# Splitting the pauses of a transform stage into short pieces, so that a second task's steps fall between them

## Chip, cores and metric

One NeuronCore of one Trainium2 chip. The metric is the device time of one execution in microseconds (us). Fast runs of the kernel before scatter by some 0.4% (1793.95 to 1801.04 us over 11 runs of one set of rounds), so two versions are compared in rounds on one chip.

In the profile PE is TensorE, PEld its weight loads, DVE VectorE, ACT ScalarE, POOL GpSimd, SPq the queue of the engine that issues most DMAs. "L646" is line 646 of the kernel.

## The reference, cut to what matters

The reference is the forward and backward pass of `x + A(layernorm(x)) + B(layernorm(x))`. `A` is a state-space convolution over 2048 steps and 576 channels, done with a Fourier transform. `B` is a gated feed-forward block of width 4608.

```python
K = jnp.einsum("dn,dnl,dn->dl", Cc, P, dB).real      # kernel of the convolution
Yf = rfft(u) * rfft(K)                               # y = irfft(Yf)[:L]
h = relu(x @ W_gate) * (x @ W_up);  out_B = h @ W_down
out, vjp = jax.vjp(f, ...);  grads = vjp(grad_out)   # all gradients are outputs
```

## The kernel before

Two programs are emitted side by side into the same engine queues. The *feed-forward* program (`ffn.gen`) has most of the matmuls (L244, L270, L298, L336, L352) and uses five PSUM tiles, `ps_mm`. The *transform* program (`s4.gen`) uses three PSUM tiles, `ps_s4`. Each is a generator that yields estimated microseconds. The main loop advances the transform generator until its sum has caught up with 0.9 of the feed-forward sum:

```python
    for us in ffn.gen(ln, final):
        ft += us
        ...
        while s4_open and stt < PACE * (ft - start):
            r = next(sgen, None)
            ...
                stt += r
```

So a "pause" is no instruction. A `yield 6.0` only means that some 6.7 us (6.0/0.9) of feed-forward instructions come next in the program.

Inside the transform program three pairs of tasks are merged by `both`: task `a` runs at its own pace, and task `b` gets a fixed share of the time `a` has used.

```python
    def both(self, a, wa, b, wb):
        ta = tb = 0.0
        for us in a:
            ta += us
            yield us
            while b is not None and tb * wa < ta * wb:
                r = next(b, None)
                ...
                    tb += r
                    yield r
        if b is not None:
            yield from b

    # gen(): the three pairs
    yield from self.both(self.p1(0, 4, 10.0), 68.0, self.params(pw), 45.0)
    yield from self.both(self.p2(0, pools, pw), 0.8 * W2, self.p1(1, 2, 3.0), W1)    # 320 : 60
    yield from self.both(self.p2(1, pools, pw), 0.8 * W2, self.p3(0, 2, 3.0), W3)    # 320 : 58
```

`p2` is the *first task* of the two long passes. For every 16 channels it emits a block of vector work and pauses, and then, for every 4 channels, it goes through smaller steps:

```python
                # ... 12 VectorE and 4 ScalarE instructions: sine and cosine, powers, A, B, X, XC ...
                yield 6.0
                for dd in range(x0, x0 + SX, DG):
                    v.tensor_tensor(vw(Y), Ap(0), Bp(1), op=ALU.mult)    # L881
                    v.tensor_tensor(vw(V), Ap(1), Bp(0), op=ALU.mult)    # L882
                    v.tensor_tensor(Y[:], Y[:], V[:], op=ALU.add)        # L883
                    yield 2.1
                    ...self.sums(...);  yield 0.8        # L932, then V L936 and Sm L937 on VectorE
                    ...self.turn(...)                    # L908 yield 0.3, L918 yield 0.4
```

`p1(1)` and `p3(0)` are the *second task*. Their steps are small. Each fills one PSUM tile (a first-stage step of `p1` two) with one or two matmuls (first stage L629, mixing L646, unmixing L656, last stage L687), copies it out on ScalarE or VectorE, and yields 0.15 to 0.7 (but for a gap of 3.0 at the start of a stage):

```python
    def mix(self, dst, src):
        for o in range(2):
            ps = self.ps()                               # one of three ps_s4 tiles
            for i in range(2):
                nc.tensor.matmul(ps[i * 64:(i + 1) * 64, :DH], lhsT=self.FM[:, o, :], rhs=src[:, i, :], ...)   # L646
            g.bal.copy(dst[:, o, :], ps[:, :DH], DH)     # ScalarE or VectorE, by a running balance
            if o == 0:
                yield 0.15
```

In the long passes the balance sent all 304 of these copies to ScalarE.

The framework orders the emitted instructions once more at build time. In the trace of the kernel before, for example, L862 of one block (643.19 us) stands on VectorE between L881 (641.99) and L882 (643.79) of another, which the source emits one right after the other.

## Time and profile before

| | before |
|---|---|
| time, median of 3 (range) | 1796.94 us (1796.20 to 1797.74) |
| PE busy | 1710 of 1792 us, 95% |
| VectorE, ScalarE busy | 1318, 1188 us |
| PE idle in the two long passes | about 33 us of 1174 us |

First, four lines of the profile page of the kernel before: the span; busy time of each engine with its instruction count; PE's busy tenths in 40 slices; and the shares of the engines in the chain that ended last.

```profile
span 1792.2 us, 41927 instructions
...
PE 1710.2 (95%) x16306; PEld 1183.1 (66%) x16449; DVE 1318.2 (74%) x2867; ACT 1188.1 (66%) x2736; POOL 204.9 (11%) x246
...
PE   7989988999999999999999999999999998999998
...
PE 64%; DVE 22%; ACT 6%; DMA 5%; issue 3%; SPq 0%; POOL 0%; ACTq 0%; DVEq 0%; POOLq 0%
```

PE is busy in nearly every slice and makes up 64% of the chain. (This trace lacks 143 matmul records, 16306 of 16449, so 1710 us is slightly low.) The next view gives busy time by stretch. After the stretch and its length come the busy time of PE, PEld, DVE, ACT and POOL, then the granted PE clock, the DMA share and GB/s.

```profile
core 0: us, PE busy (x) PEld busy (x) DVE busy (x) ACT busy (x) POOL busy (x), PEclk, DMA share, GB/s
...
96.00:296.00 200.00, 179.12 (x1437) 116.24 (x1448) 145.50 (x335) 138.94 (x336) 16.55 (x22) 0.97 0.95 300
296.00:880.00 584.00, 569.86 (x5832) 400.71 (x5879) 443.19 (x867) 408.07 (x928) 86.77 (x90) 1.00 0.72 191
880.00:1470.00 590.00, 571.27 (x5800) 400.76 (x5846) 505.42 (x1057) 401.75 (x897) 73.39 (x78) 1.00 0.69 175
```

96 to 296 us is the first pair, the rest the two long passes. PE is idle for 20.9, 14.1 and 18.7 us (length less busy). Only these stretches run through `both`, so this is all that the change can reach.

This is the timeline near one long pause in the kernel before (start, duration, engine, line, output<-input; in brackets the engine's idle time and its releaser):

```profile
654.01 0.31 PE L646 MATMUL ps_s_10652<-b_ug,FM 128*64 128x288 bf16 x2
...
654.16 0.29 PE L646 MATMUL ps_s_10656<-b_ug,FM 128*64 128x288 bf16 x2
654.28 0.29 PE L646 MATMUL ps_s_10660<-b_ug,FM 128*64 128x288 bf16 x2
...
655.63 0.42 ACT L68 CAST s_ug<-ps_s_10652 128x288 bf16<-128x288 f32 x1
...
656.11 0.31 PE L646 MATMUL ps_s_10664<-b_ug,FM 128*64 128x288 bf16 x2 [0.78 <-ACT s_ug L68]
```

Three mixing tiles stand almost together. The copy of the first (655.63) comes late on ScalarE, since ScalarE was busy without a gap from 653.50 us with two of the block's activations and three feed-forward copies, and the fourth tile, which needs that buffer, leaves PE idle for 0.78 us. Here are some of PE's waits in the long passes (303 to 1468 us): who waited for whom, total us, times, longest:

```profile
PE ps_mm L298 <- DVE T L256: 2.6, 3, 1.3
PE ps_s_10499 L908 <- ACT fC_10464 L68: 2.3, 1, 2.3
...
PE ps_s_17526 L646 <- ACT fC_17493 L68: 1.6, 1, 1.6
...
PE ps_mm L270 <- DVE T L256: 1.2, 1, 1.2
...
PE ps_s_10664 L646 <- ACT s_ug L68: 0.8, 1, 0.8
...
PE ps_mm L298 <- DVE T L261: 0.7, 3, 0.3
```

`ps_s` waits at L629, L646 and L656 are the second task's; `ps_mm` waits are the feed-forward program's. Over the passes the second task's sum to 6.9 us, the first task's (L908, L918, L932) to 8.0. (Such sums take the waits that the view lists, each over 0.15 us.) The longest single wait, 2.3 us at L908, is counted as the first task's, since a matmul of the first task waits; but what it waits for is a ScalarE copy of a second-task tile (`fC`). At 640.9 us ScalarE ran out of work and stood for 3.04 us at the block's negated copy, and the `fC` copies came after that.

### The profile page before, as it was taken

How to read it: one execution, taken by the hardware profiler on the slowest of the kernel's cores; microseconds unless marked ns; L12 is line 12 of the kernel's file. 1: busy time of each engine (PE TensorE's matmuls, PEld its weight loads, DVE VectorE, ACT ScalarE, POOL GpSimd, SP SyncE). 2: the span in 40 equal slices, each digit the busy share in tenths (PEclk: the TensorE clock that was granted, in tenths of full speed). 3: DMA queues.
4: the chain of work that ended last, by engine and by line, in shares of the span. 5: the costliest groups of instructions: out<-in, count | busy, mean ns of one | idle time of the engine just before them, and what ended most of it. 6: DMA issues, size and time to landing. Idle time of an engine off the chain costs nothing.

```text
span 1792.2 us, 41927 instructions
## 1 busy us (share of the span) xinstructions
PE 1710.2 (95%) x16306; PEld 1183.1 (66%) x16449; DVE 1318.2 (74%) x2867; ACT 1188.1 (66%) x2736; POOL 204.9 (11%) x246
## 2 busy tenths in 40 slices
PE   7989988999999999999999999999999998999998
PEld 5665556667567666766766766766676675676676
DVE  7575884677889788678787889889978963972541
ACT  5875874686588577568468658747857845864651
POOL 0200012012022011012101101101111100110000
PEclk9999999999999999999999999999999999999999
DMA  8799989678568656866857857866776578995873
GB/s 294 263 325 305 337 228 297 199 183 241 178 137 219 195 149 149 234 183 148 227 157 185 233 157 141 211 186 154 178 189 153 108 214 260 259 289 157 269 239 100
DMA packets 239003, 373.30 MB, mean 208 GB/s; under 512 B 49490, under 2 KB 153428, under 8 KB 237268
## 3 DMA queue, kind: packets, MB, share of 16 engines
q1 hardware_dynamic: 212836, 304.09, 52.8%
q0 software_dynamic: 24384, 51.92, 18.9%
q10 hardware_dynamic: 1584, 14.60, 2.2%
q8 instruction: 129, 2.11, 0.5%
q14 instruction: 70, 0.57, 0.1%
HBM read 233.10 MB, written 137.43 MB: 207 GB/s over the span
## 4 chain that ended last, share of the span: by engine, by line
PE 64%; DVE 22%; ACT 6%; DMA 5%; issue 3%; SPq 0%; POOL 0%; ACTq 0%; DVEq 0%; POOLq 0%
PE ps_mm L298 18%; PE ps_mm L244 15%; PE ps_mm L352 11%; PE ps_mm L336 8%; PE ps_mm L270 3%; DVE V L936 2%; DVE T L261 2%; DVE Sm L937 2%; DVE V L882 2%; DVE Y L883 2%; DVE Y L881 1%; DVE rg L254 1%; PE ps_mm L370 1%; DMA gT<-in_gT_dram 1%; DVE X L862 1%
## 5 line engine op out<-in xcount | busy, mean ns | idle before, releaser
L298 PE MATMUL ps_mm<-wf,T 128*128 128x288 bf16 x3456 | 481.1, 287 | 7.6 <-DVE T L256 2.6
L298 PEld LDWEIGHTS <-T 128*128 128x128 bf16 x3456 | 324.2, 98 | 97.8 <-issue 13.7
L68 ACT CAST osx<-ps_mm 128x288 bf16<-128x288 f32 x682 | 260.4, 428 | 50.0 <-PE ps_mm L298 47.2
L311 POOL DMA_DIRECT2D acc_dram<-osx x160 | 139.0, 869 | 1026.4 <-ACT osx L68 588.2
L352 PEld LDWEIGHTS <-rows 128*128 128x128 bf16 x1536 | 146.1, 98 | 96.0 <-issue 1.6
L270 PEld LDWEIGHTS <-T 128*128 128x128 bf16 x1728 | 127.0, 98 | 85.7 <-DVE T L256 4.6
L254 DVE SCALAR_TENSOR_TENSOR rg<-rg,ps_mm 128x512 bf16<-128x512 bf16 x144 | 98.3, 683 | 112.7 <-PE ps_mm L244 73.7
L244 PE MATMUL ps_mm<-xT,wd_151 128*128 128x512 bf16 x710 | 179.2, 379 | 0.8 <-issue 0.3
L244 PE MATMUL ps_mm<-gT,wd_152 128*128 128x512 bf16 x700 | 175.5, 379 | 0.8 <-DMA gT<-in_gT_dram 0.6
L244 PE MATMUL ps_mm<-xT,wd_150 128*128 128x512 bf16 x593 | 164.9, 379 | 11.8 <-DMA xT<-xT_dram 1.6
L270 PE MATMUL ps_mm<-ident_bf,T 128*128 128x128 bf16 x1728 | 157.1, 220 | 4.7 <-DVE T L256 1.6
L336 PE MATMUL ps_mm<-rows,hN 128*128 128x144 bf16 x2304 | 158.7, 227 | 0.0
L336 PEld LDWEIGHTS <-hN 128*128 128x128 bf16 x2304 | 148.3, 98 | 8.1 <-issue 5.4
L68 ACT CAST obw<-ps_mm 128x384 bf16<-128x384 f32 x103 | 49.2, 478 | 146.2 <-PE ps_mm L352 114.2
L352 PE MATMUL ps_mm<-dgN,rows 128*128 128x384 bf16 x768 | 136.8, 326 | 1.0 <-DMA rows<-xs_dram_141 1.0
L352 PE MATMUL ps_mm<-duN,rows 128*128 128x384 bf16 x768 | 135.6, 326 | 0.0
L253 ACT ACTIVATE rg<-ps_mm 128x512 bf16<-128x512 f32 x144 | 86.9, 604 | 52.2 <-PE ps_mm L244 50.3
L68 ACT CAST dhb<-ps_mm 128x512 bf16<-128x512 f32 x141 | 83.8, 594 | 49.5 <-PE ps_mm L244 47.7
L261 DVE TENSOR_TENSOR T<-dhb,rg 128x1024 bf16<-128x1024 bf16 x141 | 101.1, 717 | 18.6 <-ACT dhb L68 17.8
L244 PEld LDWEIGHTS <-wd_150 128*128 128x128 bf16 x720 | 66.0, 97 | 62.3 <-issue 3.7
L244 PEld LDWEIGHTS <-wd_151 128*128 128x128 bf16 x720 | 65.2, 98 | 60.0 <-issue 3.2
L244 PEld LDWEIGHTS <-wd_152 128*128 128x128 bf16 x705 | 63.4, 98 | 58.6 <-issue 1.6
(2506 smaller groups left out, 3042.9 us busy)
## 6 DMA issues: line engine op xcount, KB each, us to landing
acc_dram<-osx POOLq DMA_DIRECT2D x176, 288.0 KB, 5.2
gT<-in_gT_dram SPq DMA_DIRECT2D x48, 640.0 KB, 6.2
xT<-xT_dram SPq DMA_DIRECT2D x44, 640.0 KB, 5.7
rows<-in_gq_dram SPq DMA_DIRECT2D x48, 576.0 KB, 4.2
wf<-in_Wf_dram ACTq DMA_DIRECT2D x11, 1296.0 KB, 8.9
ex_dram<-exs SPq DMA_DIRECT2D x36, 320.0 KB, 4.7
ex<-ex_dram SPq DMA_DIRECT2D x36, 320.0 KB, 4.3
out_dram<-obw SPq DMA_DIRECT2D x96, 96.0 KB, 2.6
```

Source lines behind the costliest of these rows:

```text
L68: self.nc.scalar.copy(out, in_)
L244: nc.tensor.matmul(ps[:], lhsT=w[:, k, fs], rhs=rhs[:, k, :], start=(k == 0), stop=(k == NK - 1))
L253: nc.scalar.activation(rg, ps_g[:], ACT.Relu)
L254: nc.vector.scalar_tensor_tensor(upm, rg, 0.0, ps_u[:], op0=ALU.is_gt, op1=ALU.mult)
L261: nc.vector.tensor_tensor(T[:, 1:3], dhb.unsqueeze(1).to_broadcast([P, 2, JS * P]), ru[:], op=ALU.mult)
L270: nc.tensor.transpose(out=pt[:, j, :], in_=src[:, j * P:(j + 1) * P], identity=g.ident_bf[:])
L298: nc.tensor.matmul(ps[:, cs], lhsT=lt, rhs=rh, start=(i == 0), stop=(i == len(mms) - 1))
L311: nc.gpsimd.dma_start(g.acc_dram[:, t, :, :], o[:], accum_op=ALU.add)
L336: nc.tensor.matmul(ps[:, ft * 144:(ft + 1) * 144], lhsT=self.hN[:, st, ft * P:(ft + 1) * P], rhs=gq[:, st, :], start=(st == 0), stop=(st = ...
L352: nc.tensor.matmul(ps[:, :Fc], lhsT=xs[:, st, 0:P], rhs=src[:, st, :], start=(st == 0), stop=(st == ST - 1))
L882: v.tensor_tensor(vw(V), Ap(1), Bp(0), op=ALU.mult)
L883: v.tensor_tensor(Y[:], Y[:], V[:], op=ALU.add)
```

## The change

The intent: a long pause of `a` is cut in pieces of about 1 us, so that `b` is paid after each piece and not in one go after the pause.

```diff
     def both(self, a, wa, b, wb):
 
         ta = tb = 0.0
-        for us in a:
+        for us in (p for us in a for p in [us / max(1, round(us))] * max(1, round(us))):
             ta += us
             yield us
             while b is not None and tb * wa < ta * wb:
```

A pause of 6.0 becomes six of 1.0, 2.1 becomes two of 1.05, 10.0 ten of 1.0. Sums and instructions stay.

## The prediction

> **What bounds the kernel now.** TensorE: the first table of the page has PE busy 1710 of 1792 us (95%), VectorE 1318, ScalarE 1188; the granted clock is 0.995. At most 82 us are idle PE time. By stretches (the view of busy time per window) PE is idle 15 us before 96 us, 21 us from 96 to 296 (first transform beside the parameter task), 33 us from 296 to 1470 (two kernel-generating passes, each beside a transform), 14 us after. Only the two middle stretches run code that goes through `both`.
>
> **What the change does.** No instruction is added or removed. A pause is only a number in the pacing of the emission: a pause of 6.0 (36 of them, one after each block of 16 columns) becomes six of 1.0, the 144 of 2.1 two of 1.05, the 10.0 gaps ten of 1.0. Sums stay, so stages should begin and end where they did. What moves is the second task's steps. Before, after a 6.0 pause it owed 6.0*60/320 = 1.1 us and paid it in one go, 3 to 5 small steps. After, it owes 0.19 us per piece and pays about one 0.15 step each, beside the block's roughly 10 us of VectorE work (pieces of 0.49 to 0.90 us).
>
> **Gain and cost on the critical path.** A bunch makes PE wait where a fourth matmul finds the transform's three psum buffers not yet evicted. Near 654 us the timeline shows it: a row of mixing matmuls, then PE idle 0.78 us for a ScalarE copy (0.42 us each). Over 296 to 1470 us PE's waits ahead of the second task's matmuls sum to 6.9 us (mixing 3.3, first stage 2.4, unmixing 1.3): all that spreading wins directly. The first task's own matmuls wait 8 us, the feed-forward ones 10 us, mostly for VectorE's T and ScalarE; these may shift either way.
> Against it: the steps now fall just behind the block's VectorE burst, where ScalarE waits for VectorE (the sine 31 us over 27 waits, the negated copy 23 us over 22; up to 4 us at once). It takes copies in order ([...] the trace agrees: near 644 us copies stand behind a negated copy that waited 3.0 us, and PE waited 2.3 us). A step in that hole holds a psum buffer longer. I expect half of the 6.9 us won, 0 to 4 us lost again, and in the first stretch 2 us either way.
>
> **Prediction.** 1794 us, 8 times in 10 between 1784 and 1806; faster by over 2%: 2%, within 2%: 95%, slower by over 2%: 3%.
>
> **What would show it.** Same instruction counts (but for copies moved between ScalarE and VectorE); stage boundaries within 10 us; second-task PE waits in 296 to 1470 us down from 6.9 to 3 or 4 us; shorter runs of adjacent second-task matmuls; ScalarE's waits for the sine argument and the negated copy about as before; PE busy still 1710 us.
>
> **What would make it wrong.** Copies are shared out by a running balance in order of emission, and the trace's VectorE order (blocks mixed with steps) is not the program's; a small shift can put many copies behind a blocked engine. If ScalarE is stuck with second-task copies, PE waits grow by over 10 us. If the feed-forward waits on VectorE come from the bunches, the gain could reach 12 us.

## The result and the profile after

The changed kernel took 1797.8 us in the median of 6 runs (1794.71 to 1800.27), the kernel before 1797.23 us in the same rounds (1794.78 to 1799.02). The ratio is 1.0003 with a 95% interval of 0.999 to 1.0016: no difference.

The same lines of the page, after:

```profile
span 1794.1 us, 42082 instructions
...
PE 1722.6 (96%) x16449; PEld 1184.1 (66%) x16449; DVE 1319.2 (74%) x2867; ACT 1188.9 (66%) x2736; POOL 203.9 (11%) x246
...
PE   7989988999999999999999999999999998999998
...
PE 62%; DVE 20%; DMA 8%; ACT 6%; issue 3%; SPq 1%; POOL 0%; ACTq 0%; DVEq 0%; POOLq 0%
```

Busy time by stretch, after:

```profile
96.00:296.00 200.00, 178.94 (x1429) 115.59 (x1427) 144.47 (x333) 139.03 (x335) 16.48 (x22) 0.97 0.94 298
296.00:880.00 584.00, 574.34 (x5854) 399.56 (x5852) 442.42 (x866) 407.73 (x928) 83.88 (x89) 1.00 0.72 191
880.00:1470.00 590.00, 575.33 (x5884) 402.26 (x5882) 505.74 (x1056) 402.10 (x897) 75.33 (x80) 1.00 0.69 175
```

The stages lie where they did, and VectorE's and ScalarE's counts are the same. That PE's busy time is 12 us higher is mostly an effect of records: this trace has all 16449. The feed-forward matmuls of the two traces cannot be compared by busy sums. A second trace of the kernel before, with 94 more PE records in the passes than the first, showed 1136.4 us busy there against 1129.2, and this one shows 1138.7.

The same place in the stage, after (mixing tiles of the same block):

```profile
651.23 0.31 PE L646 MATMUL ps_s_10576<-b_ug,FM 128*64 128x288 bf16 x2
...
652.88 0.31 PE L646 MATMUL ps_s_10592<-b_ug,FM 128*64 128x288 bf16 x2
...
654.34 0.31 PE L646 MATMUL ps_s_10618<-b_ug,FM 128*64 128x288 bf16 x2
...
655.79 0.31 PE L646 MATMUL ps_s_10636<-b_ug,FM 128*64 128x288 bf16 x2
```

The four tiles now stand 1.4 to 1.7 us apart and none waits. The intent was met. PE's waits in the long passes, after:

```profile
PE ps_mm L298 <- DVE T L256: 3.4, 4, 1.3
PE ps_mm L270 <- DVE T L256: 2.1, 2, 1.9
PE ps_mm L298 <- DVE T L261: 1.6, 5, 0.6
PE ps_s_10499 L908 <- ACT fC_10464 L68: 1.6, 1, 1.6
...
PE ps_s_9449 L646 <- DVE V L936: 1.2, 1, 1.2
...
PE ps_s_15659 L629 <- ACT fA_15603 L68: 1.1, 1, 1.1
```

The second task's waits fell, and waits of feed-forward matmuls for VectorE's `T` rose. Sorted and summed over the passes, with the second profiles described below:

| profile | built PE order | second task | first task | feed-forward (for VectorE) | sum | length of passes |
|---|---|---|---|---|---|---|
| before | before | 6.9 | 8.0 | 11.9 (7.5) | 26.7 | 1162 |
| before, again | before | 6.5 | 8.0 | 11.2 (7.5) | 25.7 | 1163 |
| only the first pair split | before | 7.0 | 8.4 | 12.6 (7.5) | 27.9 | 1165 |
| after | after | 4.3 | 6.8 | 12.5 (10.0) | 23.7 | 1163 |
| after, again | after | 3.7 | 6.0 | 12.6 (10.0) | 22.3 | 1159 |

The rows of one order agree within 1.4 us for each kind of wait. From one order to the other the second task's waits fall by 2.8 us (means 6.8 and 4.0), the first task's by 1.7 (1.2 of it waits for `fC` copies, so for second-task tiles again), and the feed-forward ones rise by 0.7 (those for VectorE by 2.5; a wait for a load of `rows`, 0.5 to 2.0 us in each of the three profiles of the order before, is absent from the two after). Net, 3.8 us less waiting, 0.2% of the time. The timed rounds of the result (interval from 0.999) exclude a gain of more than 0.1%. So the mechanism acts, its size is at the edge of what can be measured, and part of it comes back as feed-forward waits.

The granted clock adds scatter of the same size. The first profile of the changed kernel holds one place in the passes where it fell: 0.69, 0.50, 0.50 and 0.61 in the four us from 719 to 723, after waits of PE of 0.76, 1.20 and 0.38 us between 716.1 and 719.9 us. As an estimate (1 less the granted clock, summed over the passes) that is 1.7 us of PE time lost. In the second profile of the kernel before, PE waited once for 2.25 us, up to 648.9 us, and the clock was 0.50 from 650 to 653 us; in the first profile the same wait, 2.26 us up to 645.0 us, left it at 1.00. The profile with only the first pair split holds one such place too, the second of the changed kernel none. Since it fell on both orders, nothing here ties it to the change.

### The profile page after: what moved, and what is told of

Read it like the earlier page. It is cut to its first block, busy times and chain, and to the rows that moved or that the text cites. A ratio compares the mean times of both kernels' runs of the same rounds, so it can differ in the third digit from the quotient of the medians.

```text
span 1794.1 us, 42082 instructions
## 1 busy us (share of the span) xinstructions
PE 1722.6 (96%) x16449; PEld 1184.1 (66%) x16449; DVE 1319.2 (74%) x2867; ACT 1188.9 (66%) x2736; POOL 203.9 (11%) x246
## 4 chain that ended last, share of the span: by engine, by line
PE 62%; DVE 20%; DMA 8%; ACT 6%; issue 3%; SPq 1%; POOL 0%; ACTq 0%; DVEq 0%; POOLq 0%
PE ps_mm L298 17%; PE ps_mm L244 14%; PE ps_mm L352 11%; PE ps_mm L336 7%; PE ps_mm L270 3%; DVE V L936 2%; PE ps_mm L370 2%; DVE V L882 1%; DVE T L261 1%; DVE Sm L937 1%; DVE Y L883 1%; DVE Y L881 1%; DVE rg L254 1%; DVE X L862 1%; DMA ex_dram<-exs 1%
## 5 line engine op out<-in xcount | busy, mean ns | idle before, releaser
L298 PE MATMUL ps_mm<-wf,T 128*128 128x288 bf16 x3456 | 484.5, 287 | 9.6 <-DVE T L256 3.4
L298 PEld LDWEIGHTS <-T 128*128 128x128 bf16 x3456 | 324.2, 98 | 98.1 <-issue 10.7
L352 PEld LDWEIGHTS <-rows 128*128 128x128 bf16 x1536 | 145.7, 98 | 94.6 <-issue 1.5
L244 PE MATMUL ps_mm<-xT,wd_150 128*128 128x512 bf16 x720 | 180.3, 379 | 4.0 <-ACT xT L153 1.6
L244 PE MATMUL ps_mm<-xT,wd_151 128*128 128x512 bf16 x720 | 179.9, 379 | 0.0
L244 PE MATMUL ps_mm<-gT,wd_152 128*128 128x512 bf16 x705 | 176.0, 379 | 0.7 <-DMA gT<-in_gT_dram 0.7
L352 PE MATMUL ps_mm<-dgN,rows 128*128 128x384 bf16 x768 | 137.4, 326 | 0.0
L352 PE MATMUL ps_mm<-duN,rows 128*128 128x384 bf16 x768 | 136.6, 326 | 0.0
L244 PEld LDWEIGHTS <-wd_150 128*128 128x128 bf16 x720 | 66.1, 97 | 62.0 <-issue 3.7
L244 PEld LDWEIGHTS <-wd_151 128*128 128x128 bf16 x720 | 65.2, 98 | 61.0 <-issue 3.1
L244 PEld LDWEIGHTS <-wd_152 128*128 128x128 bf16 x705 | 63.3, 98 | 59.0 <-issue 2.1
```

The costliest lines, as they stand in the source:

```text
L244: nc.tensor.matmul(ps[:], lhsT=w[:, k, fs], rhs=rhs[:, k, :], start=(k == 0), stop=(k == NK - 1))
L298: nc.tensor.matmul(ps[:, cs], lhsT=lt, rhs=rh, start=(i == 0), stop=(i == len(mms) - 1))
L352: nc.tensor.matmul(ps[:, :Fc], lhsT=xs[:, st, 0:P], rhs=src[:, st, :], start=(st == 0), stop=(st == ST - 1))
```

## The experiments

Theory one: bunches of second-task steps cost PE waits for PSUM tiles that are not evicted; spreading removes such waits, but at three buffers the kernel before had few left. Rivals: the build-time order and the queues swallow bunches whatever their size; or spreading does win, and loses it again in the hole behind the vector block, where ScalarE waits for VectorE (30.7 us in 27 waits for the sine argument in the kernel before).

A static count from the built PE orders helps below: how often four second-task tiles start within 1 us of feed-forward matmul work (L629, L646 and L656 tiles; a feed-forward matmul counted at its spacing in the trace, 0.216 us for L244, 0.122 for L298, 0.163 for L352). I call these *crowded places*. No expectation uses this count, so what it explains below it explains after the fact. Before has 11, the changed kernel none. (A recount from the traces gives the same order of the kernels and numbers up to 9 lower; 0 stays 0.) In the kernels that I counted the built order (but for single runs of four, in the kernel served at 1.0 us and in the one with one task after the other) never puts more than three second-task tiles in a row, or two when there are two PSUM tiles, however many steps the source emits at once. Runs of three number 20 before and 1 after.

### The kernels unchanged, profiled again (before_again, after_again)

No edit. One profile each.

> The kernel before, unchanged, profiled a second time: how much the PE waits of 296 to 1470 us differ between two profiles of one program. If they repeat within 1 us in total (26.8 us, of them 6.9 ahead of second-task matmuls), the drop to 4.35 and the rise of the feed-forward waits by 2 us in the changed kernel are real; if they differ by 2 us or more, they are noise.

> The changed kernel, unchanged, profiled a second time. In the two long passes (303 to 1467 us) the first profile shows second-task PE waits of 4.3 us and feed-forward waits of 13.1 us, 10.1 of them for VectorE; three profiles of the PE order of before showed 6.5 to 7.0 and 7.5. If the shift from the one to the other is real, this repeats within 0.7 us.

Measured: 1798.29 us and 1794.82 us (single runs, state unknown). The waits are in the table above: 6.5 against 6.9, and 3.7 against 4.3 for the second task; 7.5 and 7.5, 10.0 and 10.0 for VectorE. (The 13.1 and 10.1 in the expectation are an earlier sum of the waits that the table has as 12.5 and 10.0.) So the shift between kinds of waits belongs to the order, not to noise.

### Only the first pair split (split_first)

```diff
-    def both(self, a, wa, b, wb):
+    def both(self, a, wa, b, wb, split=False):
-        for us in a:
+        for us in (p for us in a for p in ([us / max(1, round(us))] * max(1, round(us)) if split else [us])):
-            yield from self.both(self.p1(0, 4, 10.0), 68.0, self.params(pw), 45.0)
+            yield from self.both(self.p1(0, 4, 10.0), 68.0, self.params(pw), 45.0, True)
```

> Pauses split only in the first pair (first transform beside the parameters). The built PE order is the same as before, so theory one (what counts is only where an instruction stands in its engine's queue, a pause is nothing in itself) expects a ratio within 0.1% of 1 and PE waits of 96 to 296 us at 20 us as before. The rival (the split frees that stretch of some of its 21 us) expects 3 us or more less there.

Measured: ratio 1.0005 (0.9989 to 1.0021), 1797.78 us. PE was idle for 20.3 us from 96 to 296 us, before for 20.9: as theory one expected. The built PE order is the same as before, instruction for instruction. The orders of VectorE, ScalarE and the issuing queue differ in a few lines. In emission the parameter task started about 9 us of pacing earlier (after a pause of 1.0, not of 10.0), yet its first load did not. DMA issues before, then after the full change:

```profile
90.19 0.32 SPq L559 DMA_DIRECT2D s_dram<-d_o_1218  x1
92.30 0.33 SPq L571 DMA_DIRECT2D raw<-in_par_dram  x1
```

```profile
90.21 0.32 SPq L559 DMA_DIRECT2D s_dram<-d_o_1218  x1
92.33 0.33 SPq L571 DMA_DIRECT2D raw<-in_par_dram  x1
```

The load `raw` stands in the issuing queue behind a store of transform constants, `d_o_1218`, and it is issued at 92.3 us in both. In the kernel before, that store waited 1.3 us for the ScalarE copy that fills its tile, and `raw` then 1.7 us for the store. The queue's order up to there is the same, so there was nothing that it could have overtaken. The pause was here only a position among the other instructions of the same queue; where none lay between, moving had no effect.

### Only the long pauses split (split_long)

```diff
-        for us in a:
+        for us in (p for us in a for p in ([us / round(us)] * round(us) if us > 5.0 and wa > 300.0 else [us])):
```

> Only the 36 pauses of 6.0 in the long passes are split in six; those of 2.1, 3.5 and the 10.0 gaps stay whole. If the long pauses are the part that matters, its waits look like those of the changed kernel (second task 4 to 5 us, feed-forward 12 to 14 us); time within 3 us of before either way. If the gain is in the short pauses, second-task waits stay near 6.9 us.

Measured: ratio 0.9987 (0.997 to 1.0004), 1794.51 us: the same. Second-task waits fell to 2.1 us (below the 4 to 5 expected), first-task 7.3, feed-forward 12.2 (9.0 for VectorE), sum 21.6; crowded places 0. So the 36 long pauses hold the whole effect on the second task. It was the lowest mean of all versions run, but the interval holds 1. It also allows a gain of 0.3%, some 5 us.

### The opposite: serve the second task late (bunch1, bunch2, bunch4)

```diff
             ta += us
             yield us
+            if b is not None and (ta * wb - tb * wa) / wa < (4.0 if wa > 300.0 else 0.0):
+                continue
             while b is not None and tb * wa < ta * wb:
```

and the same with 2.0 and 1.0 in place of 4.0.

> The opposite of the change in the two long passes: the second task is served only when it is owed 4.0 us (about once per block of 16 columns), then all at once, so runs of 10 or more small steps. Theory one (a bunch costs PE a psum wait of some tenths of a us to a us, about 7 us in all) expects second-task PE waits up from 6.9 to 15 to 30 us and the time up by 8 to 25 us. The rival (the reordering at build time and slack of the queues swallow bunches whatever their size) expects the same time within 3 us.

> As the run that served the second task at 4.0 us owed (it took 2.2% more), but at 2.0 us owed. In the built PE order the second task's runs never exceed three psum tiles in any kernel (three buffers); runs of exactly three number 1 in the changed kernel, 20 before, 43 here and 43 at 4.0. If the cost of bunches is proportional to their size, 2.0 us should cost about half of the 42 us, 15 to 25 us over before; if it is a threshold (the buffers and queues swallow small bunches), under 10 us, with second-task PE waits under 15 us.

> The second task is served when 1.0 us is owed, in both kinds of pauses (before: 1.1 us after the long pauses, 0.4 after the short ones). Known so far: 4.0 us owed costs 42 us, 2.0 costs 17, the mix of before 0 against the finest pieces. A cost in proportion to the size puts 1.0 at about 8 us (ratio 1.004 to 1.006). A threshold near 1 us (three buffers and the queued feed-forward work swallow the bunch) puts it under 4 us (ratio below 1.0025), with second-task PE waits under 12 us.

| kernel | crowded places | second-task waits | sum of waits | clock lost (estimate) | passes | time, ratio (95% interval) |
|---|---|---|---|---|---|---|
| after | 0 | 4.3 | 23.7 | 1.7 | 1163 | 1.0003 (0.999 to 1.0016) |
| before | 11 | 6.9 | 26.7 | 0 | 1162 | 1 |
| served at 1.0 us | 47 | 16.8 | 39.3 | 6.8 | 1181 | 1.0075 (1.0057 to 1.0094) |
| served at 2.0 us | 57 | 25.7 | 37.3 | 5.1 | 1179 | 1.0095 (1.0081 to 1.0109) |
| served at 4.0 us | 78 | 36.5 | 53.6 | 10.2 | 1205 | 1.0219 (1.0196 to 1.0243) |

The medians were 1814.34, 1813.56 and 1839.03 us. The rival that bunches are swallowed is refuted: they cost up to 2.2%. At 4.0 us I had expected less: second-task waits of 15 to 30 us (they were 36.5) and 8 to 25 us of time (it was about 39). At 2.0 us the cost, about 17 us, lies in the range that goes with the size. At 1.0 us it was about 13.5 us (0.75% of 1798.6), far over a threshold's 4 and more than the 8 of a cost in proportion to the size, though the interval's low end, 1.0057, just reaches into that range (1.004 to 1.006).

What follows the time better than the size owed, at 1.0 and 2.0 us, is the count of crowded places. From before to 1.0 us, 36 more of them cost 13.5 us, 0.37 us each; to 2.0 us, 46 more cost 17 us, again 0.37 each; to 4.0 us, 67 more cost 39 us, 0.59 each. This is all time, not waits alone: at 1.0 us the profiled passes are 18 us longer than the mean of the three profiles of the order before, of which 12.5 us are waits and, as an estimate, 5 to 7 us are clock. As an estimate from the 0.37 us, the 11 of the kernel before are worth 4 us, in line with the 3.8 us of waits that left it, but more than the 1.8 us (0.1%) of gain that the timed rounds allow. The change found few bunches because most of the first task is not long pauses: of about 382 us that one `p2` yields, 18 × 6.0 = 108 are, 28%. The rest is yielded in steps of at most 2.1 (but for two of 3.5), after which no more than about 0.4 us of second-task work is owed. Serving at 1.0 us gathered that rest too.

At 4.0 us the waits are no longer for PSUM tiles alone. PE's waits there (300 to 1510 us):

```profile
PE ps_s L629 <- ACT fA L68: 9.9, 6, 2.7
PE ps_s L687 <- DMA bC<-C_dk: 8.1, 6, 2.1
PE ps_s L646 <- DMA b_k<-A_k: 5.8, 1, 5.8
...
PE ps_s L656 <- DVE pr_z L672: 4.8, 8, 1.1
```

The tasks' loads (`bC`, `b_k`), which a dense bunch reaches before they have landed, and products that VectorE has not finished come on top. The lower clock, which costs time at 1.0 and 2.0 us too (an estimated 6.8 and 5.1 us, table above), is easiest to see here. Busy time in stretches of 4 us around one such bunch; the third number from the right is the granted clock:

```profile
844.00:848.00 4.00, 2.19 (x14) 0.84 (x11) 1.11 (x2) 2.03 (x5) 0.00 (x0) 1.00 0.97 211
848.00:852.00 4.00, 2.61 (x34) 2.20 (x35) 1.93 (x4) 1.59 (x4) 0.00 (x0) 0.81 0.85 262
852.00:856.00 4.00, 4.00 (x30) 2.01 (x29) 2.33 (x5) 2.34 (x4) 0.00 (x0) 0.76 0.85 247
```

Two waits of 1.1 and 2.1 us for loads, and PE then runs at 0.81 and 0.76 of its clock in the mean of 4 us; in steps of 1 us the clock is 0.75 from 850 to 851 us, 0.50 to 853 and 0.55 to 854. The kernel before shows 1.00 in every us of the passes in its first profile.

### Pay the second task before the pause (pay_first)

```diff
             ta += us
-            yield us
+            if wa < 300.0:
+                yield us
             while b is not None and tb * wa < ta * wb:
                 ...
+            if wa > 300.0:
+                yield us
```

> In the two long passes the second task is paid its share before each pause and not after it, unsplit: bunches as long as before, but just behind the block's VectorE burst, where ScalarE waits for VectorE. If the hole behind the burst is what eats the gain of spreading, second-task PE waits rise from 6.9 by 10 us or more, and the time by 8 to 20 us. If the place does not matter, waits stay at 5 to 9 us and the time within 3 us.

Measured: ratio 1.0017 (1.0001 to 1.0034), 1800.61 us; crowded places 14; second-task waits 7.3 us, first-task 4.1, feed-forward 15.2 (11.8 for VectorE). The 8 to 20 us of the hole behind the vector block did not come. What moved instead is the feed-forward program's wait for VectorE, by 4.3 us. This, like the 2.5 us of the change, fits second-task products standing earlier in VectorE's queue, ahead of `T` (the second task's copies all ran on ScalarE here too); no run takes that apart.

### Two PSUM tiles for the transforms (two_psum_before, two_psum_after)

```diff
-    g.psum_mm = pool("psum_mm", 5, space=PSUM)
-    g.psum_s4 = pool("psum_s4", 3, space=PSUM)
+    g.psum_mm = pool("psum_mm", 6, space=PSUM)
+    g.psum_s4 = pool("psum_s4", 2, space=PSUM)
```

applied to the kernel before and to the changed one.

> The kernel before with two psum banks for the transforms and six for the feed-forward work. If bunches cost time through psum buffers that are not yet evicted, one buffer less makes them dearer: second-task PE waits up from 6.9 to 12 to 25 us, time up by 5 to 25 us. If buffers are not what limits, the time stays within 3 us.

> The changed kernel with two psum banks for the transforms. Theory one (spreading saves psum waits, but at three buffers there is too little left to save) expects it 4 us or more faster than the kernel before with two banks. The rival (spreading does not act through psum waits) expects the two within 2 us.

Measured: 1831.32 us, ratio 1.019 (1.0176 to 1.0204), and 1819.73 us, ratio 1.0127 (1.0113 to 1.014); the intervals are apart, and against each other spreading is 0.6% faster (1.0127/1.019 = 0.9938). With one buffer less the very same edit wins 11 us. The loss of 34 us unsplit is more than the 5 to 25 expected. (Both kernels also have a sixth feed-forward tile, and their feed-forward waits fell to about 4 us, so what the lost buffer costs by itself is probably more than the ratios show.) PE's waits in the passes with two tiles, unsplit and then split:

```profile
PE ps_s L918 <- DVE V L936: 16.1, 16, 2.6
PE ps_s L908 <- DVE V L936: 6.1, 12, 1.5
PE ps_s L629 <- ACT fA L68: 2.1, 5, 0.9
...
PE ps_s L656 <- ACT s_k L68: 1.7, 2, 1.4
```

```profile
PE ps_s L918 <- DVE V L936: 19.2, 15, 2.5
PE ps_s L908 <- DVE V L936: 4.3, 7, 1.5
...
PE ps_s L629 <- ACT fA L68: 0.6, 3, 0.2
...
PE ps_s L656 <- ACT fC L68: 0.4, 1, 0.4
```

The second task's waits fell from 7.7 to 2.1 us in sum, and those of the first task, 29.3 and 29.5 us, did not. So my expectation of where the cost would show was wrong: the second task's waits barely rose with two tiles (6.9 to 7.7); it is the first task's turning (L918) that waits, for VectorE's `V L936`, which reads the tile to be freed (16.1 us in 16 waits unsplit). The profiled runs were 7.2 us apart (spans 1825.5 and 1818.3), 5.6 of them in these waits (40.8 and 35.2 in sum); the rest of the 11 us of the medians is not located. The clock is not the reason: it lost an estimated 3.4 us in the passes unsplit and 5.1 split.

### One task after the other (one_after_other)

```diff
-                yield from self.both(self.p2(0, pools, pw), 0.8 * W2, self.p1(1, 2, 3.0), W1)
-                yield from self.both(self.p2(1, pools, pw), 0.8 * W2, self.p3(0, 2, 3.0), W3)
+                yield from self.p1(1, 2, 3.0)
+                yield from self.p2(0, pools, pw)
+                yield from self.p3(0, 2, 3.0)
+                yield from self.p2(1, pools, pw)
```

> No interleaving of the two tasks in the long passes: the transform of half 1, then the kernel pass of half 0, then the transform back of half 0, then the kernel pass of half 1, same pace in sum. The transform alone then runs over five times as dense, with buffers for two loads only, so I expect waits for its DMA loads and psum of 20 to 60 us and the time up by 1 to 4%. If even this costs under 0.5%, order between the tasks hardly matters at all.

Measured: ratio 1.0253 (1.023 to 1.0276), 1842.19 us. As expected, PE waits for the dense transform's loads (6.5 us for `bC`, 5.9 for `b_ug`) and for evictions of its tiles (L629 9.4, L646 6.0). In 296 to 444 us, where the transform of half 1 runs alone, the granted clock was 0.93. An estimated 15 us of its passes are lost clock, against 0 or 1.7 in the order before. Merging the tasks at all is worth 45 us; splitting the pauses as the change does is worth 1.8 us at most.

### An attempt to go below both (after_deep)

The changed kernel with nine buffers and loads ahead, in place of five, for the last stage of the first transform, where PE waits 6 us for `bC`:

```diff
-            bp = self.pool(c, f"p1_c{hf}", n + 1, "right")
+            bp = self.pool(c, f"p1_c{hf}", n + 1, "right")
+            cp = self.pool(c, f"p1_cc{hf}", 9 if n == 4 else n + 1, "right")
-                Ct = bp.tile([P, 2, 1, DH], BF16, name="bC1")
+                Ct = cp.tile([P, 2, 1, DH], BF16, name="bC1")
-            Sx, cs = ..., Ahead(load_c, ST, n + 1)
+            Sx, cs = ..., Ahead(load_c, ST, 9 if n == 4 else n + 1)
```

> The changed kernel, with nine buffers and nine loads ahead in place of five in the third stage of the first transform, where PE waits 6 to 7 us for loads that stand in the queue behind weight loads. If those waits are on the critical path they fall below 2 us and the time by 3 to 6 us against the changed kernel (ratio to before 0.997 to 0.999); if PE only waits elsewhere for the same transfers, the time stays within 2 us.

Measured: ratio 0.9994 (0.9979 to 1.0009), 1795.11 us: the same. PE's waits for loads there, in the changed kernel (second profile) and then in this one:

```profile
PE ps_s L687 <- DMA bC<-C_dk: 6.2, 5, 2.0
```

```profile
PE ps_s L687 <- DMA bC<-C_dk: 3.8, 1, 3.8
...
PE ps_mm L352 <- DMA rows<-xs_dram: 1.9, 1, 1.9
PE ps_s L687 <- DMA Sx<-s_dram: 0.5, 1, 0.5
```

The wait for `bC` fell by 2.4 us but did not go. A wait of 0.5 us for `Sx` is new, and one of 1.9 us for the feed-forward program's own `rows`. The three add up to 6.2 us again, as if the wait had moved; but the three profiles of the order before show `rows` waits of 0.5 to 2.0 us as well, so that part may be scatter. The DMA engines were 0.94 busy in the mean from 96 to 296 us in the changed kernel, which fits; that bandwidth is the cause was not tested apart. No version is clear of the kernel before on the fast side.

## Why the prediction was right

The time, 1797.8 us, lies in the range of 1784 to 1806, and "within 2%" held. That alone proves little: the range is 22 us wide, and the whole effect that the text argues for is 3.5 us won and 0 to 4 lost. The central value, 1794 us, stood for a gain of some 3 us; the rounds show 0.6 us more, not less. What speaks for the prediction are its steps:

- *PE bounds, and only some 50 us of idle can be reached.* Held; PE is at 96% after.
- *No instruction added, stages stay.* Held: same counts on every engine, stage bounds within 4 us. In the first pair not even the PE order moved, which the text did not foresee; it allowed 2 us either way and got none.
- *Bunches cost PSUM waits, 6.9 us in sum, and half can be won.* The mechanism held. Second-task waits fell to 4.3 and 3.7 us, as foreseen. The two-tile pair supports that PSUM tiles are what spreading acts through: there the same edit wins 0.6% of time, and the second task's waits fall by 5.6 us. The late-served kernels show that bunches can cost 2.2%.
- *"Paid in one go, 3 to 5 small steps."* Half wrong: in the built orders counted, the bunches were broken at the number of PSUM tiles (but for the single runs of four), so the kernel before had 20 runs of three, and only 11 crowded places. The steps of the emitted source are not what PE sees.
- *"0 to 4 us lost again" behind the vector block, on ScalarE.* The size held, the place did not; that the size held was luck. ScalarE's waits for the sine argument fell (30.7 to 27.3 us), the first task's waits for `fC` copies fell too (3.2 to 2.4 and 1.6 us), and paying first cost at most 0.34%, not the 8 to 20 us that the argument implied. What came back came on the feed-forward matmuls' wait for VectorE, 7.5 to 10.0 us. That copies stood in order on ScalarE behind a waiting instruction shows in the trace (the negated copy waited 3.04 us up to 643.90 us, the `fC` copies came at 644.50 and 644.80, and PE waited 2.26 us), and the late copy at 655.63 us shown above fits it, but it didn't make this place dear.

What stays open: whether the change has a net gain of 0.1% or none. Summed waits say 3.8 us less, the timed rounds say at most 1.8 us less (0.1%). Three things could close the gap, and none was separated: matmuls that take longer without a wait being recorded, waits that other stages give back, or the lower clock, which took an estimated 1.7 us of the passes in three of the five profiles and nothing in two. Sums of PE busy time are too soft here to decide over 2 us: two profiles of the kernel before showed 1129.2 and 1136.4 us in the passes, with 94 records more in the second.

## What to carry to other kernels

Before spreading one task's steps over another's pauses, count in the built order how often more tiles stand close together than there are PSUM buffers: in these runs that count (36 more places cost 13.5 us, 0.37 us each), and not the length of the pauses in the source, told how much there was to win. A pause in emission was here only a place in each engine's queue; where the queue held nothing in between, or stood behind an unfinished store, moving a step changed nothing (`raw` at 92.30 and 92.33 us; ratio 1.0005 with only the first pair split). A cost that looks like waiting can be part clock: read the granted clock in steps of a us, not as a mean over a stage (the changed kernel shows 0.50 from 720 to 722 us, and 1.00 as the mean of 296 to 880 us). To learn whether a mechanism is absent or merely used up, overdo it the other way: serving late by 1, 2 and 4 us and taking one buffer away showed a real cost where the change itself showed none.
